# Two of four chunks of normalised rows turned to columns by DMA over DRAM instead of on TensorE, with two weight loads moved behind them

## The chip, the cores and the metric

One core of a Trainium2 chip. The metric is the time of one execution on the device in microseconds (us). The kernel before takes 214.15 us (median of 3 runs, 213.87 to 214.18). A change counts as faster or slower at 2%. A single-core run is called slow when it is over 1.5% above the fastest run of the same kernel. Such runs are listed below, but ratios use fast runs only.

## The reference, cut to what matters

```python
def reference(A_x, A_wqkv, A_wo, B_x, B_w1, B_w2, B_w3, B_w4):
    xn = _layernorm(x)                      # x: 2048 rows of 512
    s = _A_ref(xn, wqkv, wo)                # 32 heads of 16, each row sees 8 rows, 2 apart
    g = _silu(_B_ref(xn, w1, w2, w3, w4))   # gelu(layernorm(xn) @ w1), shifted groups @ w2,
    return x + s * g                        #   + gelu(layernorm(.) @ w3) @ w4
```

The heads look back by even distances, so even and odd rows (the two "parities", p = 0 and 1) are kept apart. Each parity is worked in two chunks of 512 rows: chunks 0 and 1 are the first parity, 2 and 3 the second.

## The kernel before

For each chunk TensorE (PE) needs the normalised rows as columns (`xnT`), and once more scaled by a second norm (`xn2T`). Before, PE transposes the rows (16 matmuls of 128 columns) and spreads the scale factors with one more matmul, and DVE multiplies.

```python
for c in range(1, NCH):
    if c + 1 < NCH: ln_stats(c + 1)
    stage_tr(c)            # 16 PE transposes -> xnT
    stage_w1(c - 1)
    rr_spread(c)           # one PE matmul: scale factors to all partitions
    rr_mult(c)             # DVE: xn2T = xnT * factors
    if c + 1 < NCH: ln_norm(c + 1); stage_qk(c)
    if c == 2: fill_mask(0, 0); fill_mask(0, 1)
    if c == 1: build_mask()
# ... then b(0), w1(3), b(1), qk(3), b(2), w3(0), b(3), w3(1), w3(2), w3(3), attention
```

Three things around it:

```python
def build_mask():                    # POOL builds a small table, then 2 x 16 rows of mask
    tab = sm4.tile([P, 3, P + 24], BF16, name="m_tab", tag="s4")   # pool sm4: 5 buffers, in rotation
    ...                              # two stores to DRAM, in pieces of 16 bytes
    pin(nc.sync.dma_start(out=mask_d[w].rearrange("r (g l) -> g r l", l=W), in_=rows[w]))

def fill_mask(p, w):                 # 8 DMAs of 128 KB, read from mask_d, into rows of kT or qT
    ...                              # first wanted by the attention

def stage_b(c):                      # w2 matmuls, residual, third norm, then a detour of its own:
    ...
    pin(nc.sync.dma_start(out=x1n_dram[...], in_=xn3))
    pin(nc.sync.dma_start_transpose(out=x1nT, in_=x1n_dram[...]))   # wanted by w3(c)
```

`pin` keeps an engine's instructions in the order of the program. The queue of SP (SyncE) issues all these DMAs and is such an engine: a DMA that waits holds up everything behind it.

The softmax here doesn't subtract the row's maximum and nothing guards it: scores larger than these inputs give would overflow.

## Time and profile before

| | before |
|---|---|
| time, median | 214.15 us |
| span of the profiled run | 211.9 us |
| PE busy | 201.7 us (95%) |
| DMA bytes / HBM written | 25.16 / 4.37 MB |
| start of w3(0) on PE | 65.11 us |

From the page of the profiled run: PE's busy tenths in 40 slices, PE's granted clock in the same slices, and the shares of the chain that ended last.

```profile
PE   8998999999999999999989999999999999998991
PEclk9999999999999999999999999999999999999999
PE 80%; DVE 7%; DMA 5%; ACT 2%; issue 2%; POOL 1%; SPq 1%; DVEq 0%; ACTq 0%
```

PE has no hole and a full clock. DMA is 5% of the chain. (The granted clock is the share of its full clock that the chip allows TensorE. Below, "cold" means matmuls at half of it, "warm" at the full clock.)

### The profile page before, as it was taken

Reading aid. Unit: us, or ns where it says so; the run is one execution under the profiler, and the core shown is the slowest. Engines: PE = TensorE matmul, PEld = TensorE weight load, DVE = VectorE, ACT = ScalarE, POOL = GpSimd, SP = SyncE. Lnnn points to the kernel's source line nnn. Section 1 sums busy time; section 2 is a strip of 40 time slices with the busy share of each in tenths; the row PEclk is TensorE's granted clock in tenths of the full one; section 3 lists DMA queues with packets and bytes.
Section 4 is the critical chain, followed back from the end, with each engine's and each line's share of the span. In section 5 each row is a group of like instructions: output and inputs, shape, how many; then the busy total and the mean of one; then the engine's idle time right before and its main releaser. Section 6 shows DMA issues by size and latency. Waiting matters only on the chain.

```text
span 211.9 us, 4839 instructions
## 1 busy us (share of the span) xinstructions
PE 201.7 (95%) x1978; PEld 96.5 (46%) x2007; DVE 131.0 (62%) x254; ACT 139.6 (66%) x160; POOL 55.5 (26%) x118
## 2 busy tenths in 40 slices
PE   8998999999999999999989999999999999998991
PEld 2544454544444444444444444444445544454440
DVE  6879396338839456000014666767767889688785
ACT  2098797943393625565599888788597888975310
POOL 4645774001120202000000008508039070253000
PEclk9999999999999999999999999999999999999999
DMA  5999314998240275599930003724325542445142
GB/s 152 375 395 389 117 8 6 147 145 108 99 99 3 99 198 99 140 174 126 120 39 3 0 3 61 216 80 76 114 82 141 168 103 33 129 121 107 31 147 99
DMA packets 30990, 25.16 MB, mean 119 GB/s; under 512 B 15960, under 2 KB 26424, under 8 KB 30968
## 3 DMA queue, kind: packets, MB, share of 16 engines
q1 hardware_dynamic: 27224, 19.02, 40.0%
q0 software_dynamic: 2192, 4.57, 9.1%
q10 hardware_dynamic: 1552, 1.27, 2.0%
q8 instruction: 16, 0.26, 0.6%
q14 instruction: 6, 0.05, 0.1%
HBM read 16.15 MB, written 4.37 MB: 97 GB/s over the span
## 4 chain that ended last, share of the span: by engine, by line
PE 80%; DVE 7%; DMA 5%; ACT 2%; issue 2%; POOL 1%; SPq 1%; DVEq 0%; ACTq 0%
PE w_ps L458 18%; PE w_ps L480 16%; PE qk_ps L372 10%; PE v_ps L516 7%; PE s_ps L537 7%; PE w_ps L421 6%; PE wo_ps L677 6%; PE w_ps L391 5%; PE o_ps L565 4%; DMA xn_95<-in_A_x_dram 3%; DMA oT_2427<-orw 2%; ACT prob L544 2%; DVE l1s_243 L284 1%; DVE l1s_299 L284 1%; DVE sg L686 1%
## 5 line engine op out<-in xcount | busy, mean ns | idle before, releaser
L544 ACT ACTIVATE prob<-s_ps 128x960 bf16<-128x960 f32 (+2 forms) x72 | 62.7, 925 | 11.6 <-PE s_ps L537 11.2
L480 PE MATMUL w_ps<-w_sb,h3T 128*128 128x512 bf16 (+1 forms) x174 | 43.6, 381 | 0.2 <-issue 0.2
L458 PE MATMUL w_ps<-x1nT,w_sb 128*128 128x512 bf16 (+1 forms) x173 | 38.2, 379 | 0.2
L464 ACT ACTIVATE h3T<-w_ps 128x1024 bf16<-128x1024 f32 x20 | 20.5, 1024 | 20.9 <-PE w_ps L458 20.9
L599 POOL DMA_DIRECT2D oT_1480<-orw x24 | 12.4, 525 | 61.3 <-DVE orw L572 61.3
L458 PEld LDWEIGHTS <-w_sb 128*128 128x128 bf16 (+1 forms) x176 | 17.6, 100 | 20.4
L480 PEld LDWEIGHTS <-h3T 128*128 128x128 bf16 (+1 forms) x176 | 14.7, 98 | 16.4
L521 DVE CAST v_aug_145<-v_ps 128x512 bf16<-128x512 f32 (+1 forms) x9 | 6.1, 681 | 23.1 <-PE v_ps L516 23.0
L572 DVE CAST orw<-o_ps 128x960 bf16<-128x960 f32 (+2 forms) x18 | 19.7, 1097 | 0.4 <-PE o_ps L565 0.4
L372 PEld LDWEIGHTS <-wqk_sb 128*128 128x128 bf16 x136 | 13.3, 98 | 14.3 <-issue 0.3
L599 POOL DMA_DIRECT2D oT_2427<-orw x20 | 10.1, 513 | 20.9 <-DVE orw L572 20.9
L487 DVE TENSOR_TENSOR xn_95<-w_ps,xn_95 128x512 bf16<-128x512 f32 x8 | 5.5, 692 | 16.0 <-PE w_ps L480 16.0
L372 PE MATMUL qk_ps<-xnT_149,wqk_sb 128*128 128x512 bf16 (+1 forms) x71 | 14.3, 355 | 0.3 <-DVE xnT_149 L324 0.2
L391 PE MATMUL w_ps<-xn2T,w_sb 128*128 128x512 bf16 x61 | 14.3, 379 | 0.2
L372 PE MATMUL qk_ps<-xnT_150,wqk_sb 128*128 128x512 bf16 x64 | 14.1, 379 | 0.0
L262 POOL TENSOR_SCALAR l3r<-l3m 128x4 f32<-128x4 f32 x4 | 1.0, 246 | 43.4 <-DVE l3m L270 43.4
L380 ACT ACTIVATE qT_155<-qk_ps 128x1024 bf16<-128x1024 f32 x4 | 4.1, 1030 | 9.8 <-PE qk_ps L372 9.8
L427 DVE TENSOR_TENSOR xn_96<-w_ps,xn_96 128x1024 bf16<-128x1024 f32 x4 | 4.9, 1216 | 8.3 <-PE w_ps L421 8.3
L421 PE MATMUL w_ps<-w_sb,hT_160 128*128 128x512 bf16 x32 | 9.5, 379 | 0.0
L516 PE MATMUL v_ps<-wv_sb,xnT_150 128*128 128x512 bf16 (+1 forms) x28 | 8.9, 383 | 0.4
L391 PEld LDWEIGHTS <-w_sb 128*128 128x128 bf16 x64 | 6.1, 98 | 6.8
L421 PE MATMUL w_ps<-w_sb,hT_159 128*128 128x512 bf16 x30 | 9.1, 379 | 0.1
(161 smaller groups left out, 328.8 us busy)
## 6 DMA issues: line engine op xcount, KB each, us to landing
w_sb<-in_B_w_dram SPq DMA_DIRECT2D x1, 1376.0 KB
w_sb<-in_B_w_dram SPq DMA_DIRECT2D x1, 1280.0 KB
wqk_sb<-in_A_wqkv_dram SPq DMA_DIRECT2D x2, 512.0 KB
w_sb<-in_B_w_dram SPq DMA_DIRECT2D x2, 512.0 KB
xn_96<-in_A_x_dram SPq DMA_DIRECT2D x4, 256.0 KB
xo_1598<-in_A_x_dram POOLq DMA_DIRECT2D x4, 256.0 KB, 3.9
xo_2228<-in_A_x_dram POOLq DMA_DIRECT2D x4, 256.0 KB, 3.7
out_dram<-xo_1598 SPq DMA_DIRECT2D x3, 256.0 KB
```

The costliest lines, as they stand in the source:

```text
L372: nc.tensor.matmul(pt[:, b, h : h + n], lhsT=wqk_sb[:, dt, nt * P : (nt + 1) * P], rhs=xnT[p][:, dt, k * CH + h : k * CH + h + n], start=( ...
L391: nc.tensor.matmul(pt[:, b, :], lhsT=w1_sb[:, dt, g * P : (g + 1) * P], rhs=xn2T[:, dt, :], start=(dt == 0), stop=(dt == ND - 1),)
L421: nc.tensor.matmul(pt[:, j, :], lhsT=w2_src(p, g, m0), rhs=w2_sb[:, g, :], start=(g == 0), stop=(g == ND - 1),)
L458: nc.tensor.matmul(pt[:fs, ft % 2, :], lhsT=w3_sb[:, dt, ft * P : ft * P + fs], rhs=x1nT[:, dt, :], start=(dt == 0), stop=(dt == ND - 1),)
L464: last["gelu"] = nc.scalar.activation(h3T[:, 2 * a : 2 * a + 2, :], pt, AF.Gelu_apprx_tanh)
L480: nc.tensor.matmul(pt, lhsT=h3[c][:fs, ft, jj * P : (jj + 1) * P], rhs=w4_sb[:fs, ft, :], start=(ft == 0), stop=(ft == NF - 1),)
L516: nc.tensor.matmul(vp[:nk, :], lhsT=xnT[p][:, dt, k0 : k0 + nk], rhs=wv_sb[:, dt, :], start=(dt == 0), stop=(dt == ND - 1),)
L537: nc.tensor.matmul(st[:nk, b, i * nq : (i + 1) * nq], lhsT=kT[p][e][r : r + 32, dt, k0 : k0 + nk], rhs=qT[p][e][r : r + 32, dt, q0 : q0 + ...
L544: nc.scalar.activation(prv[:nk, 2 * h : 2 * h + 2], st[:nk, :, 0 : 4 * nq], AF.Exp, scale=SCALE)
L572: pin(nc.vector.tensor_copy(out=orw[p][:, :, :, q0 - ra : q0 - ra + nq], in_=op[:, :, 0 : 4 * nq].rearrange("p j (s q) -> p j s q", q=nq),))
L599: (nc.scalar if (p, r) == (1, 2) and jj else nc.gpsimd).dma_start(out=oT[p][DH * hh : DH * (hh + 1), :, ra : ra + rw], in_=orw[p][32 * cg ...
L677: nc.tensor.matmul(pt, lhsT=oT[p][:, dt, i * P : (i + 1) * P], rhs=wo["sb"][:, dt, lo:hi], start=(dt == 0), stop=(dt == ND - 1),)
```

## The change

The intent: take the transposes and factor matmuls of chunks 2 and 3 off PE. The rows, plain and scaled, go to DRAM and come back through the transposing DMA. The V and w4 weights, wanted only by the attention, are loaded after chunk 2's transposes.

```diff
+    def dma_tr(c):
+        x_c = xn[p][:, k * TPC : (k + 1) * TPC, :]
+        pin(nc.sync.dma_start(out=xn_dram[0, cs, :]..., in_=x_c))
+        xn2 = sm4.tile([P, TPC, D], BF16, name="xn2", tag="s4")
+        ...                                             # DVE: xn2 = x_c * r2, four instructions
+        pin(nc.sync.dma_start(out=xn_dram[1, cs, :]..., in_=xn2))
+        pin(nc.sync.dma_start_transpose(out=xnT[p][:, :, cs], in_=xn_dram[0, cs, :]))
+        xn2Ts[c] = sm4.tile([P, ND, CH], BF16, name="xn2T", tag="s4")
+        pin(nc.sync.dma_start_transpose(out=xn2Ts[c], in_=xn_dram[1, cs, :]))
 ...  (the loop is written out; order of the stages now:)
+    ln_stats(2); stage_tr(1); stage_w1(0); rr_spread(1); ln_norm(2)
+    dma_tr(2)
+    late_loads()                                        # wv, w4: were in the first loads
+    rr_mult(1); stage_qk(1); ln_stats(3); ln_norm(3)
+    dma_tr(3)
+    build_mask()
+    stage_w1(1); stage_qk(2)
+    fill_mask(0, 0); fill_mask(0, 1)
+    stage_w1(2)
     stage_b(0)
     stage_w1(3)
```

More of the change, by code (lines that the diff above doesn't have):

```diff
@@ L80 @@
     x1n_dram = dram.tile([S, D], BF16, name="x1n_dram")
+    xn_dram = dram.tile([2, M, D], BF16, name="xn_dram")
     def bigt(shape, name):
@@ L148 @@
     nc.sync.dma_start(out=w3_sb, in_=B_w3.rearrange("(dt q) f -> q dt f", q=P))
-    wv_sb = const.tile([P, ND, D], BF16, name="wv_sb")
-    nc.sync.dma_start(out=wv_sb, in_=wqkv_v[:, :, 2 * D : 3 * D])
-    w4_sb = midt([P, NF, D], "w4_sb")
-    nc.sync.dma_start(
-        out=w4_sb[:, 0 : NF - 1, :],
-        in_=B_w4[0 : (NF - 1) * P, :].rearrange("(ft q) n -> q ft n", q=P),
-    )
-    nc.sync.dma_start(out=w4_sb[0:FL, NF - 1, :], in_=B_w4[(NF - 1) * P : F, :])
     nc.scalar.preload_act_table_set("gelu_apprx_tanh_and_others")
@@ L243, in fill_mask, with late_loads @@
                 )
+    late = {}
+    def late_loads():
+        late["wv"] = const.tile([P, ND, D], BF16, name="wv_sb")
+        pin(nc.sync.dma_start(out=late["wv"], in_=wqkv_v[:, :, 2 * D : 3 * D]))
+        late["w4"] = midt([P, NF, D], "w4_sb")
+        pin(
+            nc.sync.dma_start(
+                out=late["w4"][:, 0 : NF - 1, :],
+                in_=B_w4[0 : (NF - 1) * P, :].rearrange("(ft q) n -> q ft n", q=P),
+            )
+        )
+        pin(nc.sync.dma_start(out=late["w4"][0:FL, NF - 1, :], in_=B_w4[(NF - 1) * P : F, :]))
     NV = 2
@@ L331, in stage_tr @@
             transposes(c, h)
+    def dma_tr(c):
+        p, k = c // 2, c % 2
+        cs = slice(k * CH, (k + 1) * CH)
+        x_c = xn[p][:, k * TPC : (k + 1) * TPC, :]
+        pin(nc.sync.dma_start(out=xn_dram[0, cs, :].rearrange("(i q) d -> q i d", q=P), in_=x_c))
+        r2 = r2s.pop(c)
+        xn2 = sm4.tile([P, TPC, D], BF16, name="xn2", tag="s4")
+        for j in range(TPC):
+            pin(
+                nc.vector.tensor_scalar(
+                    out=xn2[:, j, :], in0=x_c[:, j, :], scalar1=r2[:, j : j + 1], scalar2=None, op0=ALU.mult
+                )
+            )
+        pin(nc.sync.dma_start(out=xn_dram[1, cs, :].rearrange("(i q) d -> q i d", q=P), in_=xn2))
+        pin(nc.sync.dma_start_transpose(out=xnT[p][:, :, cs], in_=xn_dram[0, cs, :]))
+        xn2Ts[c] = sm4.tile([P, ND, CH], BF16, name="xn2T", tag="s4")
+        pin(nc.sync.dma_start_transpose(out=xn2Ts[c], in_=xn_dram[1, cs, :]))
     def rr_spread(c):
@@ L480, in half @@
                     nc.tensor.matmul(
-                        pt, lhsT=h3[c][:fs, ft, jj * P : (jj + 1) * P], rhs=w4_sb[:fs, ft, :],
+                        pt, lhsT=h3[c][:fs, ft, jj * P : (jj + 1) * P], rhs=late["w4"][:fs, ft, :],
                         start=(ft == 0), stop=(ft == NF - 1),
@@ L516, in values @@
                 nc.tensor.matmul(
-                    vp[:nk, :], lhsT=xnT[p][:, dt, k0 : k0 + nk], rhs=wv_sb[:, dt, :],
+                    vp[:nk, :], lhsT=xnT[p][:, dt, k0 : k0 + nk], rhs=late["wv"][:, dt, :],
                     start=(dt == 0), stop=(dt == ND - 1),
@@ L716 @@
     stage_qk(0, [1, 2, 3])
-    for c in range(1, NCH):
-        if c + 1 < NCH:
-            ln_stats(c + 1)
-        stage_tr(c)
-        stage_w1(c - 1)
-        rr_spread(c)
-        rr_mult(c)
-        if c + 1 < NCH:
-            ln_norm(c + 1)
-            stage_qk(c)
-        if c == 2:
-            fill_mask(0, 0)
-            fill_mask(0, 1)
-        if c == 1:
-            build_mask()
+    ln_stats(2)
+    stage_tr(1)
+    stage_w1(0)
+    rr_spread(1)
+    ln_norm(2)
+    dma_tr(2)
+    late_loads()
+    rr_mult(1)
+    stage_qk(1)
+    ln_stats(3)
+    ln_norm(3)
+    dma_tr(3)
+    build_mask()
+    stage_w1(1)
+    stage_qk(2)
+    fill_mask(0, 0)
+    fill_mask(0, 1)
+    stage_w1(2)
     stage_b(0)
```

## The prediction

> **What bounds the kernel now.** I read four views of the kernel before: the page's chain of work that ended last, the timeline of PE, the timeline of the SP queue, and what that queue waited for.
>
> The chain, in order of time, for the part that the change touches:
>
> ```profile
> 20.47 0.70 DVE xn2T L343 x4
> 21.61 6.91 PE qk_ps L372 x32
> 28.51 0.89 PE tr_ps L321 x16
> 29.67 3.19 PE w_ps L391 x14
> 33.09 6.91 PE qk_ps L372 x32
> 40.00 0.89 PE tr_ps L321 x16
> 41.16 3.19 PE w_ps L391 x14
> ...
> 62.74 2.54 PE w_ps L421 x11
> 65.28 8.20 PE w_ps L458 x38
> ```
>
> Columns: start, time, engine and line. From 21 us on PE carries the end without a hole, so a PE instruction that goes is time won, as long as its replacement arrives in time. The two tr_ps rows are the PE transposes of chunks 2 and 3 (the second parity).
>
> SP issues nearly all DMAs, in order. Its timeline (start, time of the issue):
>
> ```profile
> 12.28 5.42 SPq L156 DMA_DIRECT2D w_sb<-in_B_w_dram  x1
> 29.59 0.38 SPq L232 DMA_DIRECT2D mask_d<-m_rows_424  x1
> 30.37 0.60 SPq L232 DMA_DIRECT2D mask_d<-m_rows_436  x1
> 35.46 1.74 SPq L240 DMA_DIRECT2D kT_151<-mask_d  x4
> 37.30 2.85 SPq L240 DMA_DIRECT2D kT_152<-mask_d  x4
> 40.19 4.02 SPq L240 DMA_DIRECT2D qT_155<-mask_d  x4
> 44.29 3.58 SPq L240 DMA_DIRECT2D qT_156<-mask_d  x4
> 55.02 0.40 SPq L436 DMA_DIRECT2D x1n_dram<-xn_662  x1
> 57.97 2.09 SPq L441 DMA_TRANSPOSE x1nT<-x1n_dram  x1
> ```
>
> The sixteen mask fills hold SP from 35.46 to 47.87. The store and transpose of the first x1 chunk, which feed the w3 matmuls (L458), come behind them at 55.02. Those fills now have 7 us of slack. Read in half-microsecond windows, the DMA engines move fill data until about 52.3, the store's data from 56.0 to 57.4, and the transpose's data from 59.4 to 62.0. The w3 matmuls start at 65.11, nearly 3 us later.
>
> The mask that the fills read is built on POOL, early:
>
> ```profile
> 22.78 1.12 POOL L191 IOTA m_tab<- 128x75 bf16 x4
> 30.04 0.31 POOL L230 TENSOR_SCALAR m_rows_436<-ones_bf,mg 128x8 bf16<-128x8 bf16 x1
> ```
>
> And SP's waits (who for whom: us, times, longest):
>
> ```profile
> SPq L240 <- DMA mask_d<-m_rows_424: 4.4, 1, 4.4
> SPq L441 <- DMA x1n_dram<-xn_662: 2.4, 1, 2.4
> ```
>
> **What the Trainium skill says.** "TensorE: Matmul & The Clock Gate", Part 1, gives 55.6 ns start to start for warm matmuls of 128 columns. The trace agrees: the first tr_ps starts at 28.35, the w1 matmuls at 29.24, 0.89 us for 16. The same part says that the array falls to half clock after an idle window of about 3.4 us and needs sustained work to come back. The trace shows the cold side at its start only, with warm-up matmuls 0.43 us apart from 1.45 to 5.72, against 0.216 us later; it has no such hole afterwards. "DMA: Bandwidth & Descriptors", Rules for kernel authors, says that a DMA reading what an earlier one wrote must wait for its completion; the trace shows this price, 57.97 - 55.02 = 2.95 us from store to transpose. The same page, Queues, rings and completion order, says descriptors are consumed in ring order on each DMA engine, so one SP transfer queues behind another's bytes. This agrees with the fill data flowing 4.4 us past their last issue.
>
> **The change, part by part.** *Removed from PE:* two times 16 transposes at 0.89 us = 1.78, and two spread matmuls (L348; 32.70 to the next matmul at 32.93, 0.22 us each) = 0.44. Sum 2.2 us on the path, about 1%. DVE loses casts (1.25 us a chunk), diagonals (0.75) and the wide multiply (1.23) and gains four scalings a chunk (as L297, 1.38); ACT loses 0.6 a chunk. None of it is on the path.
>
> *Chunk 2 by DMA.* DVE finishes the diagonals of chunk 1 at 21.16; ln_norm(2) runs to 22.55. The store issues at 22.6 and lands 2.95 later, 25.55. Scaling waits for the second factor on POOL (22.82) and ends 24.2; its store lands at 27.2. The first transpose issues at 25.55 and, as x1's did (57.97 to 62.0 plus an estimated 0.4 for completion), lands 4.4 later, 30.0. PE, without transposes, reaches w1(1) at 28.35 and qk(2) at 31.8: in time by 1.8. The second transpose (issue 27.65, data behind the first) lands near 32.4; w1(2) comes at 38.7. Hidden.
>
> *The moved loads.* Wv and w4 are 1.9 MB, about 5.0 us at the 385 GB/s seen in the load phase. They stood in the stream at 18 to 23; now they issue at 29.8 and move from about 31.9 to 36.9. Their first readers are beyond 105 us, so by themselves they cost nothing.
>
> *Chunk 3.* DVE: rr_mult(1) to 25.4, statistics (2.75 as at 16.56 to 19.30) to 28.2, POOL's root 1.53 to 29.7, ln_norm to 31.1, second factor at 31.7, scaling to 33.1. The two stores sit in the rings behind wv and w4: data 36.9 to 38.3 and 38.3 to 39.7, the second landing at 40.2. Transposes issue at 38.85 and 40.95; xn2T lands near 45.7, where PE wants it for w1(3) at 45.65. Even.
>
> *The mask, which the diff only seems to reorder.* In the built program the mask table takes the buffer of chunk 3's scaled rows: POOL's first iota waits for that store to land. So the start moves from 22.78 to 40.2, 17.4 us. The rest keeps its lengths: to the first mask store, 29.59 - 22.78 = 6.8; to the fills, 35.46 - 29.59 = 5.9; fills start at 53.0. Sixteen issues take 12.4 (35.46 to 47.87), to 65.4. The x1 store of chunk 0 is ready on DVE near 52 but stands behind them in SP's order. Its data follow the fills' data: 65.4 + 4.4 to drain + 1.4 + 0.5 = 71.7; transpose 4.4 more: 76.1. I take 75.8, since rings that drain first start the store first.
>
> PE's program order has qk(3) and b(2) before w3(0), and is through with them at 65.1 - 2.2 = 62.9. It then idles about 13 us. From there PE is full until 106 as before, and the other stores and transposes have slack again (the next lands near 82, wanted after 90). The shift is 75.8 - 65.1 = +10.7; the 2.2 saved is already inside, swallowed by the wait. After such a hole PE restarts cold. If it is cold for 3.4 (the page) to 5 us (the start of this trace), at half rate, that loses 1.7 to 2.5; I take 2.0. Sum: +12.7, or 226.8; I round to 226.5 because the earlier steps can err more on the short side.
>
> **Rivals.** *(a) All hidden.* The masks are first read at 107, so if their lateness stayed off SP's path, the 2.2 us would be kept: 212. For it: PE fills the chain, and the transposes have time. Against: x1's store is behind the fills in the same in-order queue, and 7 us of slack does not hold 17. *(b) Loads don't delay the stores.* If chunk 3's scaled store lands right after scaling, 33.1 + 2.95 = 36.05, everything behind it is 4.1 earlier: w3 at 71.7, +6.6, plus 2 cold: about 222.5. Against: wv and w4 issue first on the same rings. *(c) PE waits for chunk 2 or 3 itself*, at qk(2) or w1(3): one or two us, but before the larger hole, so the latter swallows it; 227. *(d) More delay:* POOL slower beside DVE (one L220 took 1.44, the other 0.46), or masks slower: up to 230.
>
> **Range and chances.** The early landing bounds the low side, (d) the high side: 221 to 230. Slower by over 2% means above 218.4, a net loss over 4.3 us. That fails only if the store is not held behind the fills or the mask starts before about 33; no step supports that. Slower 0.93, same 0.05, faster 0.02.
>
> **What would show it.** In the changed profile: PE's qk(2) starts near 31.8 without a wait on DMA; the first iota of m_tab on POOL near 40, released by the scaled store; first fill near 53, last issued near 65; x1's first store behind it; the first w3 matmul near 76, with about 13 us idle before it, put down to the x1nT transfer; then matmuls 0.43 apart for some us. DMA bytes grow by some 4 MB. I am wrong if iota starts before 33, if fills take clearly less than 12 us, or if PE has no hole over 5 us between qk(3) and w3.

## The result, and the profile after

| | before, same chip | after |
|---|---|---|
| median | 214.01 us | 228.42 us |
| runs | 213.33 to 214.18 | 227.22, 224.47 fast; 229.65, 229.62 slow |
| ratio of fast runs | | 1.056 (1.044 to 1.068) |
| DMA bytes / HBM written | 25.16 / 4.37 MB | 29.34 / 6.47 MB |

A ratio here is the mean time of one kernel's fast runs over that of the other's of the same rounds, so it is not quite the ratio of the medians. The changed kernel is slower. Its page, profiled in a fast run with a span of 225.4 us, has these rows in answer to those of before:

```profile
PE   8998999949980399999999899999999999998991
PEclk9999999999998579999999999999999999999999
PE 61%; DMA 19%; DVE 8%; POOL 6%; issue 2%; SPq 1%; ACT 1%; POOLq 0%; ACTq 0%
```

Two holes stand in PE's row, at slices 9 and 13 to 14 (a slice is 5.6 us), and the clock falls in the second. DMA and POOL have come into the chain. The chain in order of time (start, time, what), cut to its long pieces, shows how (m_tab is the mask table, m_rows the mask rows):

```profile
33.35 8.61 DMA xn_dram<-xn_448
...
42.12 1.12 POOL m_tab L185 x4
...
47.74 6.35 DMA mask_d<-m_rows_467
...
54.14 4.76 DMA kT_147<-mask_d
58.92 6.63 DMA qT_151<-mask_d
...
65.62 6.61 DMA x1n_dram<-xn_625
...
72.29 4.28 DMA x1nT<-x1n_dram
...
78.36 10.60 PE w_ps L485 x40
```

This is one string of transfers: the scaled rows of chunk 3 take 8.6 us to land; then POOL may overwrite their buffer with the mask table; the mask goes to DRAM; the fills read it; the first x1 store stands behind the fills; its transpose feeds w3. PE's own timeline (start, time, group, and in brackets the idle time before it with what ended it) has the other side:

```profile
32.24 7.07 PE L399 MATMUL qk_ps<-xnT_146,wqk_sb 128*128 128x512 bf16 x32
39.14 3.62 PE L418 MATMUL w_ps<-xn2T,w_sb 128*128 128x512 bf16 x15
...
49.15 3.63 PE L418 MATMUL w_ps<-xn2T,w_sb 128*128 128x512 bf16 x16 [2.94 <-DMA xn2T<-xn_dram]
...
76.70 1.44 PE L485 MATMUL w_ps<-x1nT,w_sb 128*128 128x512 bf16 x3 [10.11 <-DMA x1nT<-x1n_dram]
```

Chunk 2's columns (qk(2) at 32.24, w1(2) at 39.14) came without a wait. Chunk 3's scaled columns cost 2.94 us before w1(3), and the first x1 columns 10.11 us before w3(0). The weight loads of the first 13 w3 matmuls, up to 81.77, are 0.427 us apart, twice the 0.216 of warm ones.

### The profile page after: what moved, and what is told of

The parts are those of the page before. It is cut to its first block, busy times and chain, and to the rows that moved or that the text cites. A ratio compares the mean times of both kernels' runs of the same rounds, so it can differ in the third digit from the quotient of the medians.

```text
span 225.4 us, 4784 instructions
## 1 busy us (share of the span) xinstructions
PE 202.4 (90%) x1944; PEld 95.0 (42%) x1973; DVE 127.2 (56%) x248; ACT 138.4 (61%) x158; POOL 55.0 (24%) x118
## 2 busy tenths in 40 slices
DMA packets 41421, 29.34 MB, mean 130 GB/s; under 512 B 24344, under 2 KB 36856, under 8 KB 41400
## 3 DMA queue, kind: packets, MB, share of 16 engines
q10 hardware_dynamic: 1552, 1.27, 1.9%
HBM read 16.15 MB, written 6.47 MB: 100 GB/s over the span
## 4 chain that ended last, share of the span: by engine, by line
PE 61%; DMA 19%; DVE 8%; POOL 6%; issue 2%; SPq 1%; ACT 1%; POOLq 0%; ACTq 0%
PE w_ps L507 18%; PE w_ps L485 18%; PE v_ps L543 7%; PE s_ps L564 7%; PE wo_ps L704 6%; PE o_ps L592 4%; DMA xn_dram<-xn_448 4%; DMA qT_151<-mask_d 3%; DMA x1n_dram<-xn_625 3%; DMA xn_96<-in_A_x_dram 3%; DMA mask_d<-m_rows_467 3%; DMA kT_147<-mask_d 2%; DMA x1nT<-x1n_dram 2%; PE w_ps L448 2%; DVE l1s_239 L292 1%
## 5 line engine op out<-in xcount | busy, mean ns | idle before, releaser
L485 PE MATMUL w_ps<-x1nT,w_sb 128*128 128x512 bf16 (+1 forms) x173 | 40.6, 395 | 10.4 <-DMA x1nT<-x1n_dram 10.1
L485 PEld LDWEIGHTS <-w_sb 128*128 128x128 bf16 (+1 forms) x176 | 18.2, 104 | 32.7 <-issue 14.1
L626 POOL DMA_DIRECT2D oT_1443<-orw x24 | 12.4, 524 | 61.3 <-DVE orw L599 61.3
```

The costliest lines, as they stand in the source:

```text
L485: nc.tensor.matmul(pt[:fs, ft % 2, :], lhsT=w3_sb[:, dt, ft * P : ft * P + fs], rhs=x1nT[:, dt, :], start=(dt == 0), stop=(dt == ND - 1),)
L626: (nc.scalar if (p, r) == (1, 2) and jj else nc.gpsimd).dma_start(out=oT[p][DH * hh : DH * (hh + 1), :, ra : ra + rw], in_=orw[p][32 * cg ...
```

## The experiments

Ten kernels ran. All gave correct results, and each was timed beside the kernel before on the same chip. Three questions: which link of the string holds w3, whether the detour over DRAM costs anything by itself, and whether an order exists in which it pays. The medians and ranges below take in slow runs (one each in own_tab, mask_late_alone and mask_act, two in warm_hole, as two of the changed kernel's four), so compare runs by the last column; there the changed kernel has 1.056 (1.044 to 1.068).

| run | this, median (range) | before, median | ratio of fast runs (95%) |
|---|---|---|---|
| fills_late | 220.80 (219.27–222.06) | 213.35 | 1.034 (1.029–1.040) |
| own_tab | 230.98 (228.32–232.03) | 213.35 | 1.078 (1.071–1.085) |
| loads_late | 222.87 (222.24–224.43) | 213.35 | 1.047 (1.043–1.051) |
| warm_hole | 227.53 (224.19–231.01) | 213.35 | 1.053 (1.049–1.056) |
| mask_early2 | 223.25 (222.41–224.72) | 213.52 | 1.045 (1.041–1.049) |
| mask_late_alone | 218.46 (217.55–220.82) | 213.52 | 1.022 (1.018–1.026) |
| mask_act | 224.43 (222.36–225.95) | 213.71 | 1.053 (1.048–1.057) |
| mask_act_split | 218.75 (218.48–219.17) | 213.71 | 1.024 (1.022–1.026) |
| mask_behind | 211.36 (211.14–211.58) | 213.51 | 0.990 (0.987–0.992) |
| order_only | 211.24 (211.18–212.01) | 213.62 | 0.990 (0.988–0.991) |

At the 2% rule the last two are the same as the kernel before, mask_late_alone is unclear, and the rest are slower.

**fills_late: the fills moved behind the x1 stores.**

```diff
-    fill_mask(0, 0)
-    fill_mask(0, 1)
     stage_w1(2)
     stage_b(0)
+    fill_mask(0, 0)
     ...
     stage_b(3)
+    fill_mask(0, 1)
```

> The changed kernel with the sixteen mask fills moved behind the x1 transposes in the queue: eight after the first x1 transpose, eight after the last. My theory (the x1 store stands behind the fills in SP's order): the first x1 store issues near 53, its transpose lands near 60, PE has no hole before w3(0), no cold stretch, and the time falls from 227 to about 215.2, which is before minus 2.2 for the PE work plus 2.9 for the wait at w1(3) plus 0.4. Rival (the cost is the DMA detour itself, or the moved loads): the hole before w3 stays, 224 to 228.

It measured 220.80. By the ratios of fast runs the loss fell from 5.6% to 3.4%, about 4.6 us, less than expected. The hole before w3(0) is gone: the first x1 store went out at 53.15 instead of 65.62, and w3(0) started at 69.40 without a wait. So the fills in front of that store are a link of the string. The wait at w1(3), counted as 2.9 us, took 3.43. What I missed is that w1(3) then ran cold (16 matmuls in 6.37 us instead of 3.62):

```profile
49.38 6.37 PE L418 MATMUL w_ps<-xn2T,w_sb 128*128 128x512 bf16 x16 [3.43 <-DMA xn2T<-xn_dram]
```

The eight k fills now stood before the second x1 store. And the third norm of chunk 2, which DVE was free to order, slid behind chunk 3's work, so that its store went out at 87.35 and PE waited another 2.59 us for it before w3(2), cold again (88 matmuls in 20.85 us, about 19.2 at the warm rate).

**own_tab: the mask table given a buffer of its own.** The first form, a new buffer in another pool, did not fit in SBUF. This one uses a part of a buffer that only the attention needs.

```diff
-        tab = sm4.tile([P, 3, P + 24], BF16, name="m_tab", tag="s4")
+        tab = orwp.tile([P, 2 * ND * RW], BF16, name="m_tab", tag="orw")[:, 0 : 3 * (P + 24)]...
```

> The changed kernel with the mask table in a buffer that nothing else uses so early. If the shared buffer alone sets the fills' start (my prediction as written), the mask is ready on POOL near 38 instead of 48.5, fills start near 44, w3(0) near 66, about 215. If the mask stores then wait in SP's order behind the transposes of chunk 3 (issued 40.6 to 45.0 in the changed kernel), they issue near 45.0 instead of 47.7: w3(0) near 74, about 224.5, a gain of 2.7 only. I expect the second.

It measured 230.98, slower than the changed kernel (1.078 against 1.056, the intervals apart). Two things happened. The scheduler, now free, put the whole mask build at the start of POOL, where it delayed the first norm (first root at 7.78 instead of 4.59) and made PE start cold, some 3 us. And the mask stores still went out only at 49.13, because they stood in SP's order behind chunk 3's two transposes, the second issued at 45.29. A short wait was enough for a cold w1(3):

```profile
51.08 5.31 PE L420 MATMUL w_ps<-xn2T,w_sb 128*128 128x512 bf16 x16 [2.11 <-DMA xn2T<-xn_dram]
```

So the buffer is one bound on the mask, and SP's order a second one right behind it. The expected gain needs both to go.

**loads_late: V and w4 loaded after chunk 3's transposes.**

```diff
     dma_tr(2)
-    late_loads()
     ...
     dma_tr(3)
+    late_loads()
```

> The changed kernel with the wv and w4 loads issued after chunk 3's transposes instead of before its stores. If the loads stand in front of chunk 3's stores in the rings, the scaled store lands near 36.3 instead of 42.0, the first iota moves there, and the wait of 2.9 us at w1(3) goes. The mask stores then come behind the loads' data (to about 46), so the fills start near 51.5 and w3(0) near 74: about 224.5. If the rings do not hold the stores back, nothing moves: 227.

It measured 222.87, a little better than expected. Against the changed kernel the gain in time is not clear: the ratios of fast runs are 1.047 and 1.056, and their intervals overlap. The trace is clear. SP's timeline (start, issue time):

```profile
31.95 0.38 SPq L346 DMA_DIRECT2D xn_dram<-xn  x1
...
34.90 1.95 SPq L356 DMA_TRANSPOSE xnT<-xn_dram  x1
```

Chunk 3's first store landed 2.95 us after its issue. In the changed kernel the same pair stood at 32.43 and 40.63, so 8.2 us, behind the loads' data. The wait at w1(3) is gone. The hole before w3(0) is 7.70 instead of 10.11, since the mask stores now stood behind the loads (issue at 42.27, taking 7.08), and w3(0) ran cold (44 matmuls in 12.49 us, against 9.66 warm).

**warm_hole: 44 unused matmuls in the hole before w3(0).** They work on constants, so the result is the same.

```diff
     stage_b(2)
+    keep = psb("keep_ps")                 # nobody reads it
+    for _ in range(44):
+        pin(nc.tensor.matmul(keep, lhsT=ones_bf[:], rhs=ones_bf..., start=True, stop=True))
     stage_w3(0)
```

> The changed kernel with 44 unused matmuls (about 9.5 us warm) after b(2), inside PE's hole before w3(0), so that PE is not idle. If the slow first matmuls of w3(0) (0.427 us apart for 5.4 us) come from the idle hole, they go, w3(0) takes 9.5 instead of 12.1 us, the mean clock of the record goes back to 0.99 or more, and the time falls by 2.6 to about 224.6. If they come from anything else, the time stays at 227 or grows.

It is inconclusive in time: 224.19 and 225.07 fast, 229.98 and 231.01 slow, beside 224.47 and 227.22 fast for the changed kernel. The intervals of the two ratios overlap. In its profile w3(0) ran warm (44 matmuls in 9.66 us), as expected, but w1(3) ran cold instead after a wait of 2.66 us (5.31 us for 16), which it did not in the changed kernel's profile (the last section shows why).

```profile
66.81 9.66 PE L769 MATMUL keep_ps<-ones_bf 128*128 128x512 bf16 x44
76.31 9.66 PE L485 MATMUL w_ps<-x1nT,w_sb 128*128 128x512 bf16 x44
```

The unused matmuls also held w3(0) back. The first x1 transpose was issued at 68.37; at the 4.3 us that it took in the changed kernel it landed near 72.7 (an estimate), while they ran until 76.31. So this run can't weigh the cold loss in time. It is seen in the traces only (2.6 us). Runs some 5 us apart remain: the mean clock is 0.992 and 0.997 in the fast two, 0.982 and 0.985 in the slow two. What else differs between them stays open, as one profile is kept for each kernel.

**mask_late_alone: the kernel before, with the mask built one round later.** No transpose over DRAM, loads where they were.

```diff
         if c == 2:
+            build_mask()
             fill_mask(0, 0)
             fill_mask(0, 1)
-        if c == 1:
-            build_mask()
```

> The kernel before, with one line moved: the mask is built in the round of chunk 2, just ahead of its fills, instead of the round of chunk 1. No transpose over DRAM, loads where they were. Theory (a late mask is enough for the loss): mask stores at about 40 to 42, landed by 47, fills until 57 to 58, first x1 store behind them, its transpose landed at 67 to 70, a hole of 3 to 6 us before w3(0)[...]; time 217 to 222. Rival (without the DMA transposes a late mask is absorbed): 213.0 to 214.5, no hole.

It measured 218.46, 4.9 us over the kernel before. From SP's and PE's timelines:

```profile
37.72 2.76 SPq L232 DMA_DIRECT2D mask_d<-m_rows  x2
...
56.45 0.40 SPq L436 DMA_DIRECT2D x1n_dram<-xn  x1
64.06 2.30 SPq L441 DMA_TRANSPOSE x1nT<-x1n_dram  x1
```

```profile
68.79 11.34 PE L458 MATMUL w_ps<-x1nT,w_sb 128*128 128x512 bf16 x44 [3.47 <-DMA x1nT<-x1n_dram]
```

The mask stores are 8.1 us later than before (29.59). The x1 store is only 1.4 us later (55.02 before), but lands after 7.6 us instead of 2.95, because the fills' data are still moving. PE waits 3.47 us and loses 1.7 more to a cold start (11.34 against 9.66). So a late mask alone, without the detour, costs about 2% (1.8 to 2.6).

**mask_early2: the mask built early, its stores between chunk 2's and chunk 3's transfers.**

```diff
+        with tc.issue_after(root[2].ins):     # not before r2 of chunk 2
             for i, o, v in (...): gp.iota(...)
 ...
     dma_tr(2)
-    late_loads()
+    build_mask()                              # table in its own buffer, as in own_tab
     ...
     dma_tr(3)
-    build_mask()
     ...
     stage_b(0)
+    late_loads()
```

> The changed kernel with the transposes over DRAM kept for both chunks, but the mask built early again: its table takes a view of a buffer of another pool, its five iotas are held on POOL behind the r2 of chunk 2 (about 22.8 us) so that they don't come at the start, its two stores stand on SP between chunk 2's and chunk 3's transposes, the fills stay where they were, and the V and w4 loads go behind the first x1 transpose. Theory (the detour over DRAM is hidden; what costs is the lateness of the mask and of the fills, and the loads in front of chunk 3's store): mask stores at about 30, landed by 37; chunk 3's transposes landed by about 42; the eight fills done by about 50; first x1 store near 52, its transpose landed by 62, no hole before w3(0), no clock at half speed there, no wait at w1(3); time 211 to 214.5 against 213.4 of the kernel before, so the same or up to 1% faster. Rival (the detour itself, with its 4 MB more through the DMA engines, is the loss): 219 or more, with waits at w1(2) and w1(3). Rival (loads behind the first x1 transpose delay the next ones): first w3 on time, a wait of 3 us or more before the second or third.

It measured 223.25 where 211 to 214.5 was expected: my theory was wrong in one link. The mask stores went out at 30.86, but chunk 3's first store, issued at 34.16, let its transpose go only at 43.07, 8.9 us later, with no weight load in front of it. Only 64 KB of mask stood there. PE waited 4.76 us at w1(3), the fills ran late again, and w3(0) waited 4.38 us.

```profile
30.86 1.72 SPq L229 DMA_DIRECT2D mask_d<-m_rows  x2
34.16 0.38 SPq L350 DMA_DIRECT2D xn_dram<-xn  x1
...
43.07 3.19 SPq L360 DMA_TRANSPOSE xnT<-xn_dram  x1
```

Either the queue's order delays a store, or small pieces slow the DMA engines for everybody.

**mask_act: those two stores on ACT's queue.**

```diff
-            pin(nc.sync.dma_start(out=mask_d[w]..., in_=rows[w]))
+            pin(nc.scalar.dma_start(out=mask_d[w]..., in_=rows[w]))   # called after stage_w1(1)
```

> mask_early2 with one thing moved: the two mask stores (pieces of 16 bytes) go out from ACT's queue behind the two gelus of w1(1), at about 34 us, instead of standing on SP's queue ahead of chunk 3's two stores. Theory (a store behind other data in the same queue lands 8 to 9 us after its issue instead of 3, whether that data is 1.9 MB of weights as in the changed kernel or the 16-byte pieces of the mask as in mask_early2): chunk 3's stores landed by about 39, its second transpose by 45, the wait of 4.76 us at w1(3) gone or under 1 us and its matmuls warm (3.6 us for 16); the sixteen fills run about 42 to 58, so the first x1 transpose lands at 63 to 66 and leaves a hole of 0 to 3 us before w3(0), without cold matmuls. Time 213 to 217, against 223.25 of mask_early2. Rival (the queue doesn't matter, the DMA engines are simply full of small pieces): chunk 3's stores still land 8 us late, 221 to 224.

The rival held: 224.43. ACT issued the mask stores from 32.33, and on SP:

```profile
33.69 0.38 SPq L353 DMA_DIRECT2D xn_dram<-xn  x1
...
43.89 1.84 SPq L363 DMA_TRANSPOSE xnT<-xn_dram  x1
```

The store took 10.2 us with its own queue free. In windows of one microsecond from 33 to 36 us the DMA engines were busy for 0.54, 0.95 and 1.26 of the window by the view's count, yet moved 19 to 24 GB/s; in the changed kernel, with the weight loads and chunk 3's stores on them, they moved 237 to 386 from 33 to 41 us. The mask stores are 4096 packets of 16 bytes (the packets of ACT's queue rose from 1552 to 5680). So here they held up the store, though they came by another queue.

**mask_act_split: mask_act with, in addition, q fills behind the first x1 transpose, V and w4 loads behind the last, and the additions and the third norm pinned on DVE.**

```diff
     stage_qk(2)
     fill_mask(0, 0)
-    fill_mask(0, 1)
     stage_w1(2)
     stage_b(0)
-    late_loads()
+    fill_mask(0, 1)
     ...
     stage_b(3)
+    late_loads()
```

> mask_act, with the eight q fills put behind the first x1 transpose, the V and w4 loads behind the last one, and the additions and the third norm of the second stage held in program order on DVE. Theory (with the queue in front of the first x1 store free as well, nothing of the detour is left on the path, and the 2.2 us of PE work that it takes away show): first x1 store at about 52 to 54, its transpose landed by 61, no hole over 0.5 us before any w3 or w1, no slice at half clock after the first 10 us; time 211 to 213, 0 to 1% under the kernel before of the same chip. Rival (4 MB more through the DMA engines shift waits to the later stages): a hole of 2 us or more before the second, third or fourth w3, or later where V or w4 are wanted, and 215 or more.

It measured 218.75. From w3(0), at 71.18, on there is no wait left in PE's timeline up to the attention, so the second part of the theory holds. But w1(3) still waited 4.91 us and ran cold (6.42 us for 16), because the small pieces still met chunk 3's store. Those two account for 7.7 us (4.91, and 6.42 - 3.62).

**mask_behind: transfers in the order of their deadlines.** Chunk 3's stores and transposes go before the mask stores, all on SP. Half of the k fills go before the first x1 store and half after its transpose. The loads follow the second x1 transpose, the q fills the fourth. The early mask and the DVE work pinned in mask_act_split stay. (The diff leaves out the lines taken out.)

```diff
     dma_tr(3)
+    store_mask(mask_rows)
     stage_w1(1)
     stage_qk(2)
+    fill_mask(0, 0, (0,))       # 4 of the 8 k fills
     stage_w1(2)
     stage_b(0)
+    fill_mask(0, 0, (1,))       # the other 4
     stage_w1(3)
     stage_b(1)
+    late_loads()
     ...
     stage_b(3)
+    fill_mask(0, 1)             # the 8 q fills
```

> The transposes over DRAM kept for both chunks, the mask rows computed early as in mask_act_split (POOL done at about 31 us), and the transfers put in the order of their deadlines, all on SP's queue: chunk 3's two stores and two transposes first, then the two mask stores, then four of the k fills, the first x1 store and its transpose, the other four k fills, the second x1 store and transpose, the V and w4 loads, the third and fourth, and last the eight q fills, which only the attention wants. Theory (nothing of the detour itself costs time; a store lands late when 16-byte pieces or 1.9 MB of loads are on the engines, whichever queue they came by): chunk 3's stores landed 3 to 4 us after their issue, its second transpose by 45, no wait at w1(3) and its 16 matmuls in 3.6 us; mask stores at 39 to 41; the first x1 transpose landed by 62.5, no hole over 0.5 us before any w3; no slice under full clock after the start. Time 210.5 to 213 against 213.6 of the kernel before, ratio 0.985 to 1.0. Rival (the detour costs time by itself in some way not yet seen, or the loads and fills only move their hole to the second to fourth w3 or to the start of the attention): 215 or more, with a wait of 2 us or more in one of those places.

It measured 211.36, all six runs within 0.5 us. That is 1.0% under the kernel before (0.987 to 0.992): clear of noise, but the same at the 2% rule. The chunk 3 store landed in 2.83 us (33.26 to 36.09), w1(3) started at 45.76 without a wait, w3(0) at 63.03. So the detour costs nothing by itself in this order, and the PE work that it takes away shows: w3(0) is 2.08 us earlier than before (65.11).

**order_only: the same, with the early mask taken back.** The table is again in the buffer of chunk 3's scaled rows and built after them.

```diff
-        tab = orwp.tile(...)                  # and without issue_after
+        tab = sm4.tile([P, 3, P + 24], BF16, name="m_tab", tag="s4")
 ...
     dma_tr(3)
-    store_mask(mask_rows)
+    store_mask(build_mask())
```

> mask_behind with the early mask taken back: the mask table again in the buffer of chunk 3's scaled rows, built after them as in the changed kernel. What is left against the changed kernel is the order of transfers alone (loads behind the second x1 transpose, fills in three parts, the second stage's DVE work in program order). Theory A (the order alone decides; the table's wait on the buffer is harmless once the loads no longer stand in front of the store that frees it): scaled store of chunk 3 landed by 37, first iota at about 37, mask stores at 42 to 43, landed by 49, first four k fills at 49 to 51, first x1 store at 52 to 53, its transpose landed by 62.5, no hole; 210.5 to 212.5, the same as mask_behind within 0.5 us. Theory B (an early mask is needed as well): the x1 store stands behind the four fills until 55 or later, a hole of 1 to 4 us before w3(0), perhaps cold; 212.5 to 216.

It measured 211.24, the same as mask_behind: theory A. SP's timeline, then PE's:

```profile
31.93 0.38 SPq L350 DMA_DIRECT2D xn_dram<-xn  x1
...
34.83 2.11 SPq L360 DMA_TRANSPOSE xnT<-xn_dram  x1
...
42.23 1.33 SPq L229 DMA_DIRECT2D mask_d<-m_rows  x2
47.96 1.74 SPq L237 DMA_DIRECT2D kT<-mask_d  x4
52.94 0.40 SPq L469 DMA_DIRECT2D x1n_dram<-xn  x1
56.60 2.01 SPq L474 DMA_TRANSPOSE x1nT<-x1n_dram  x1
```

```profile
46.37 3.62 PE L422 MATMUL w_ps<-xn2T,w_sb 128*128 128x512 bf16 x16
...
63.64 9.66 PE L491 MATMUL w_ps<-x1nT,w_sb 128*128 128x512 bf16 x44
```

And from its page, the granted clock and the chain:

```profile
PEclk9999999999999999999999999999999999999998
PE 84%; DVE 6%; DMA 3%; SPq 1%; ACT 1%; issue 1%; POOL 1%; ACTq 0%
```

Neither PE group has a bracket: nothing waited. The mask is as late as the buffer allows (stores at 42.23, against 29.59 before), yet harms nobody, because only four fills of 1.74 us stand before the x1 store, and the loads no longer delay the store that frees the buffer. The wait on the buffer, which the prediction found, was real. It did not have to be undone. The changed kernel's bytes, transposes and waits on buffers are all still in this kernel; the order of its transfers (with the second stage's DVE work pinned to go with it) is what differs. No run has the order without the pins, or the pins alone. For the first x1 store they make little difference: it went out at 52.94 here and at 53.15 in fills_late, which has none.

## Why the prediction was right

The prediction, 226.5 with 221 to 230, met 228.42 (the two fast runs: 224.47 and 227.22), and the chain went as it said. Its steps, against the profiled run of 227.22:

| step | predicted | measured |
|---|---|---|
| qk(2), w1(2) by DMA | 31.8, 38.7, no wait | 32.24, 39.14, no wait |
| first mask iota, behind the scaled store | 40.2 | 42.12, released by that store |
| first mask store, first fill | 47.0, 53.0 | 47.74, 54.14 |
| sixteen fill issues | 12.4, until 65.4 | 10.8, until 64.93 |
| x1 store landed | 71.7 | 72.23 |
| w3(0) | 75.8 | 76.70 |
| idle before it | about 13 | 10.11, and 2.94 before w1(3) |
| cold loss | 2.0 | 2.6 |

That the sum comes so close is in part luck: the mask began 1.9 us late and its fills took 1.6 us less, and the runs themselves lie 5 us apart. One sign of being wrong, "if fills take clearly less than 12 us", was near: they took 10.8.

*Removed from PE.* The 2.2 us are right. They are invisible in the changed kernel, as predicted ("swallowed by the wait"), and they are what mask_behind and order_only gain: 2.15 and 2.38 us by the medians.

*Chunk 2.* Hidden, as predicted.

*Chunk 3, the term that was mis-sized.* "xn2T lands near 45.7 [...] Even" was 3.45 us short: it let PE go at 49.15. The first transpose issued at 40.63 instead of 38.85, since the loads were issued 0.66 us later (30.46) and loads and stores together did not hold 385 GB/s: between 33 and 41 us the one-microsecond windows show 237 to 386, and 119 just before. The second transpose issued at 42.11 instead of 40.95, and needed 7.0 us from there instead of the 4.75 assumed, behind the first one's data. By itself this wait did not move the end: it lies before the larger hole, which shrank by as much. Rival (c) had said so.

*The moved loads.* "By themselves they cost nothing" is right in that nobody waits for the weights. Their cost is in what stood behind them, which the prediction put into chunk 3's step. Rival (b), the case of loads that don't delay the stores, was put at 222.5; loads_late, which makes it true, measured 222.87. The match is partly luck, since there the mask stores stood behind the loads instead.

*The mask.* The wait on the buffer, the place of the fills and the x1 store behind them are confirmed by the chain, and by mask_late_alone and fills_late from two sides. The sizes erred by 0.5 to 1.9 us, in both directions. The prediction took the wait on the buffer as the root. That is right for what the changed kernel did, but own_tab shows that SP's order would hold the mask nearly as long, and order_only that the wait may stay.

*The cold start.* The traces show 2.6 us after the 10 us hole: from w3(0)'s first matmul to the next stage it takes 12.1 us (76.70 to 88.79), against 9.5 before (65.11 to 74.61). The time of warm_hole does not confirm it. A start 11.6 us later and 2.6 us cold make 14.2; the profiled runs differ by 13.5, so 0.7 us came back later, which was not traced.

*Rivals.* (a), all hidden, failed on the in-order queue, as argued against it. With another order of the same work it is what happens: it put 212, and order_only measured 211.24.

Open: part of the spread of the changed kernel's runs (224.5 to 229.7). mask_behind and order_only, without a wait there, spread by 0.4 and 0.8 us, but mask_act_split, with 4.91 us of waiting, by 0.7 as well. So waits alone don't explain it, and which transfer or cold start varies was not shown. One candidate is where a wait falls against the clock's windows (last section).

## What to carry to other kernels

When a transfer is added or moved, list what stands behind it in its queue, and what shares the DMA engines with it: the harm came to a store that the change never touched, 30 us later. Put transfers in the order of their deadlines before shortening any of them; here the order, with the DVE work held to it, turned a loss of 5.6% into a gain of 1.0%. And look in the built program for buffers that now have another owner, since a rotation of buffers can tie a small table to a slow store.

## What the Trainium skill lacked or had wrong

- "TensorE: Matmul & The Clock Gate", Part 1, gives the idle window as about 3.4 us and a rule against gaps longer than that. The rule does not hold here as it stands. Waits of 2.11 us (own_tab), 2.59 and 3.43 (fills_late), 2.66 (warm_hole) and 3.47 (mask_late_alone) were followed by cold matmuls, while 2.94 (changed kernel) and 3.72 (mask_act, before w3(0)) were not.
- What decides is how much idle time falls into one window. Read in slices of a quarter microsecond, the granted clock was at half for 3.4 us (own_tab, warm_hole, mask_late_alone, mask_early2), 6.8 (fills_late, mask_act, mask_act_split) or 10.2 (changed kernel, own_tab, loads_late). Where one trace has several falls, they lie 7, 12 or 14 times 3.41 us apart. So in these traces the clock changes on a fixed grid of 3.41 us, which fits the page's remark that the window runs freely. Laid on this grid, every window at the full clock with 2.07 us or more of idle PE ended in a fall, and none with 1.91 or less did (the program's start and end left out; matmul ends as the profile models them). The 2.94 us of the changed kernel were split 1.64 and 1.29 and the 3.72 of mask_act 1.91 and 1.81, and neither made a fall; the 2.66 of warm_hole and the 2.11 of own_tab each lay in one window. In own_tab the clock fell at 51.60, after the matmuls had begun again at 51.08. The page's rule lacks this: a shorter gap can cost and a longer one can be free.
- The same part gives a warm-up budget of about 3.4 us. After the hole of 10.11 us the matmuls were cold for about 5.3 us (76.70 to 82.00). On the grid, the clock came back at the end of the first window that was full of work; a window with 1.05 us of idle time in it (loads_late, 70.46 to 73.87) did not bring it back.
- "DMA: Bandwidth & Descriptors", Why small descriptors are slow and Issuing engines are not separate DMA queues, says that small pieces carry overhead and that all queues interleave on the same engines, which mask_act agrees with. It has no size for what a bystander pays: 4096 pieces of 16 bytes (64 KB) made a store of 512 KB take 8.9 us from issue to its transpose's issue in the same queue and 10.2 us from another, against 2.8 to 3.0 us alone. That is at least as much as 1.9 MB of weight loads in front of it cost (8.2 us in the changed kernel, 8.4 to 8.7 in warm_hole, own_tab and fills_late).
- Pages give a rate for a transposing DMA, but none has what two of 512 x 512 in a row take, from the first one's issue to the matmul that wants the second: 7.0 to 8.6 us in the seven runs where PE waited for it (40.63 to 49.15 in the changed kernel), against 4.3 for a single one (72.29 to 76.56).
